# Float64 weights to fp32: exponent and mantissa by floating-point arithmetic, or a shifted upper word plus an integer addition

## The chip, the core and the metric

The kernel runs on one core of a Trainium2 chip. That core has TensorE (matrix products; PE in the profile, with PEld for its weight loads), VectorE (DVE) and ScalarE (ACT) for elementwise work, GpSimd (POOL), and SyncE (SP), which here issues DMA transfers between HBM and the on-chip memory SBUF. The metric is the device time of one execution in microseconds; lower is better.

## What is computed

An attention block without a softmax feeds a two-layer network. In short:

```python
# q, k, v: (8 batches, 8 heads, 576 rows, 64)
kv  = einsum('bhsd,bhse->bhde', k, v)
o   = einsum('bhsd,bhde->bhse', q, kv)
x   = o / sqrt(mean(o*o, -1) + 1e-6) * g_norm        # then (4608 tokens, 512)
h   = x @ w_in                                       # (4608, 2048)
g   = h * erf(softplus(h))
out = g @ w_out                                      # (4608, 512), fp32
```

`w_in` (512 x 2048) and `w_out` (2048 x 512) arrive as **float64**. [...] each weight reaches the kernel as two 32-bit words, and the kernel makes an fp32 number out of them. The change is in that step alone.

## The kernel before

The tokens are worked off in nine groups (512 rows of each of the eight batches, and a last group with the 64 rows left of each); group T=0 begins while the weights are still being fetched. The weights come in 18 pieces, in the order in which they are needed: four of `w_in` with 128x512 numbers, six of `w_in` and eight of `w_out` with 128x1024. Each piece is loaded raw (`load_w`), taken apart (`w_split`) and put together (`w_join`); the plan of the program places these three steps between the other work.

A float64 has a sign bit, 11 exponent bits and 20 mantissa bits in its upper word, and 32 mantissa bits in its lower word. The kernel before builds two factors: `e`, an fp32 power of two with the sign, and `m`, an fp32 number from 1 to 2; their product is the weight.

```python
    def w_split(which, f, k):
        hi = w_raw[which, f].rearrange("p (n two) -> p n two", two=2)[:, :, 1]
        e = early.tile([P, G * k], I32, name="w_e", tag="w_e", bufs=2)
        m = early.tile([P, G * k], I32, name="w_m", tag="w_m", bufs=2)
        nc.vector.tensor_scalar(out=e, in0=hi, scalar1=20, scalar2=0x7FF,          # L207
            op0=ALU.logical_shift_right, op1=ALU.bitwise_and)
        nc.scalar.activation(e, e, AF.Relu, scale=float(1 << 23), bias=exp_col)    # L215
        nc.vector.tensor_scalar(out=m, in0=hi, scalar1=0xFFFFF, scalar2=None,      # L216
            op0=ALU.bitwise_and)
        nc.scalar.activation(m.bitcast(FP32), m, AF.Identity, scale=2.0**-20, bias=1.0)  # L219
        w_cv[which, f] = e, m

    def w_join(which, f, k):
        # hi, lo: the upper and lower words of the raw piece, every second word
        nc.vector.scalar_tensor_tensor(out=e, in0=hi, scalar=-(1 << 31), in1=e,    # L226
            op0=ALU.bitwise_and, op1=ALU.bitwise_or)
        nc.vector.scalar_tensor_tensor(out=m, in0=lo, scalar=2.0**-52, in1=m,      # L230
            op0=ALU.mult, op1=ALU.add)
        nc.vector.tensor_tensor(out=out_, in0=e, in1=m, op=ALU.mult)               # L240
```

(Written more tightly than in the kernel; `out_` is the piece's place in `w_in_sb` or `w_out_sb`.) The plan around the first group, cut:

```python
    w_rounds = {
        1: ("split",),
        2: ("join", "load", "split"),
        3: ("join", "load"),
        5: ("split",),
        6: ("split", "join", "load", "join", "load"),
    }
    ...
    for i in range(NP + 3):                       # NP = 4 pairs of heads
        for piece, p in ((0, i), (1, i - 1), (4, i - 3), (3, i - 2)):
            if 0 <= p < NP:
                first[p][piece]()                 # 0 products, 1 apply, 3 mean, 4 norm of pair p
        if i == 1:
            for _ in range(RAW - 2):
                w_next("load")
            ...
        for what in w_rounds.get(i, ()):
            w_next(what)
```

The norm of a head pair, whose lines stand between the conversion's in the profile:

```python
            nc.scalar.activation(r, ms, AF.Ln, bias=eps_col)                       # L358
            nc.scalar.activation(r, r, AF.Exp, scale=-0.5)                         # L359
            nc.scalar.activation(u, r, AF.Square)                                  # L360
            ...
            nc.vector.scalar_tensor_tensor(out=u, in0=ms, scalar=EPS, in1=u,       # L366
                op0=ALU.add, op1=ALU.mult)
            nc.vector.scalar_tensor_tensor(out=u, in0=u, scalar=3.0, in1=r,        # L369
                op0=ALU.subtract, op1=ALU.mult)
            ...
            nc.vector.scalar_tensor_tensor(out=x, in0=st.pop("o"), scalar=gm_col,  # L378
                in1=u, op0=ALU.mult, op1=ALU.mult)
```

The hidden products that take the converted weights, block by block (blocks 0 and 1 together, then one by one):

```python
                nc.tensor.matmul(plain[i],                                         # L692
                    lhsT=w_in_sb[:, c, i % FC * P : i % FC * P + P],
                    rhs=xT[T][:, c, :], start=(c == 0), stop=(c == KC - 1))
```

Of the kernel before, what the change touches and what calls it, by code (L numbers as in the profile page):

```python
# [39 lines left out]
FP32 = mybir.dt.float32  # L40
FP32R = mybir.dt.float32r
I32 = mybir.dt.int32
U32 = mybir.dt.uint32
AF = mybir.ActivationFunctionType
ALU = mybir.AluOpType
# [15 lines left out]
def kernel(  # L61
# [10 lines left out]
    nc = tc.nc  # L72
    P = 128
# [11 lines left out]
    const = ctx.enter_context(tc.tile_pool(name="const", bufs=1))  # L85
# [67 lines left out]
    for i in range(2):  # L153
        nc.gpsimd.dma_start(
            out=g_col[i * D : i * D + D, :], in_=g_norm.rearrange("(d one) -> d one", one=1)
# [16 lines left out]
    for i in range(2):  # L172
        nc.vector.memset(mean_f[i * D : i * D + D, i * D : i * D + D], 1.0 / D)
    nc.vector.tensor_copy(out=mean_w, in_=mean_f)
    exp_col = const.tile([P, 1], FP32, name="exp_col")
    nc.vector.memset(exp_col, -896.0 * (1 << 23))
    eps_col = const.tile([P, 1], FP32, name="eps_col")
    nc.vector.memset(eps_col, EPS)
    bd_kv = const.tile([P, 2, P], FP32, name="bd_kv")
# [6 lines left out]
    w_raw, w_cv = {}, {}  # L186
    RAW = 4

    def load_w(which, f, k):
# [6 lines left out]
        else:  # L196
# [2 lines left out]
                in_=moe_w_out.rearrange("(t p) f -> p t f", p=P)[:, f : f + k, :],  # L199
            )  # L200

    def w_split(which, f, k):

        hi = w_raw[which, f].rearrange("p (n two) -> p n two", two=2)[:, :, 1]
        e = early.tile([P, G * k], I32, name="w_e", tag="w_e", bufs=2)
        m = early.tile([P, G * k], I32, name="w_m", tag="w_m", bufs=2)
        nc.vector.tensor_scalar(  # L207
            out=e,
            in0=hi,
            scalar1=20,  # L210
            scalar2=0x7FF,
            op0=ALU.logical_shift_right,
            op1=ALU.bitwise_and,
        )
        nc.scalar.activation(e, e, AF.Relu, scale=float(1 << 23), bias=exp_col)  # L215
        nc.vector.tensor_scalar(  # L216
            out=m, in0=hi, scalar1=0xFFFFF, scalar2=None, op0=ALU.bitwise_and
        )
        nc.scalar.activation(m.bitcast(FP32), m, AF.Identity, scale=2.0**-20, bias=1.0)  # L219
        w_cv[which, f] = e, m  # L220

    def w_join(which, f, k):
        raw, (e, m) = w_raw.pop((which, f)), w_cv.pop((which, f))
        hi = raw.rearrange("p (n two) -> p n two", two=2)[:, :, 1]
        lo = raw.bitcast(U32).rearrange("p (n two) -> p n two", two=2)[:, :, 0]
        nc.vector.scalar_tensor_tensor(  # L226
            out=e, in0=hi, scalar=-(1 << 31), in1=e, op0=ALU.bitwise_and, op1=ALU.bitwise_or
        )
        m = m.bitcast(FP32)
        nc.vector.scalar_tensor_tensor(  # L230
            out=m, in0=lo, scalar=2.0**-52, in1=m, op0=ALU.mult, op1=ALU.add
        )
        e = e.bitcast(FP32)
        if which == "in":
            out_ = w_in_sb[:, :, f * P : (f + k) * P]
            e, m = (t.rearrange("p (c f) -> p c f", c=KC) for t in (e, m))
        else:
            out_ = w_out_sb[:, f : f + k, :]
            e, m = (t.rearrange("p (c f) -> p c f", c=k) for t in (e, m))
        nc.vector.tensor_tensor(out=out_, in0=e, in1=m, op=ALU.mult)  # L240


    w_order = sorted(
# [6 lines left out]
    def w_next(what):  # L250
        i = w_at[what]
        if i < len(w_order):
            w_at[what] = i + 1
            {"load": load_w, "split": w_split, "join": w_join}[what](*w_order[i][1:])
# [389 lines left out]
    for n in range(FIRST * FC + 1):  # L644
        T, f = divmod(n, FC)
# [108 lines left out]
    def part(h, half):  # L754
        return h[:, :, half * 2 * P : half * 2 * P + 2 * P]
# [31 lines left out]
    for m in range(first_batch, batches + 1):  # L787
# [73 lines left out]
        for j in range(J):  # L861
# [13 lines left out]
            for half in due_halves:  # L875
                nc.vector.tensor_tensor(  # L876
                    out=part(h, half), in0=part(h, half), in1=part(s, half), op=ALU.mult
# [38 lines left out]
```

## Time and profile before

| | |
|---|---|
| time, median of 3 runs | 944.46 us (944.22 to 944.83) |
| span of the profiled execution | 942.4 us |
| conversion, first raw word read to last weight written | 14.4 to 125.0 us |
| VectorE operations of the conversion | 18 each of L207, L216, L226, L230, L240 |
| ScalarE operations of the conversion | 18 each of L215, L219 |

In the profile a line such as L207 is a line of the kernel before; `out<-in` names the tiles written and read. The chain that ended last follows, from the last instruction backwards, what released each instruction; time on it is time that sets the end. The clock that TensorE was granted was 1.00 in every stretch of the span.

### The profile page before, as it was taken

The page shows a single profiled execution, that of the slowest core. Times are in us where ns is not written, and L with a number is a line of the kernel's source. Part 1 is how long each engine was busy: PE and PEld are TensorE (multiplying, and loading weights), DVE is VectorE, ACT ScalarE, POOL GpSimd, SP SyncE. Part 2 cuts the span into 40 slices and gives each one's busy share as a digit, 9 for nine tenths or more (in the row PEclk, how much of TensorE's full clock was granted, in tenths as well). Part 3 has the DMA queues.
Part 4 walks back from the last instruction along what each step waited for, and adds up shares of the span by engine and source line. Part 5 has one row for each costly group of instructions (what it writes and reads, how often), then busy time and mean ns, then how long its engine had stood idle before and what let it go on. Part 6 is the DMA issues. An engine that isn't in the chain of part 4 may idle for free.

```text
span 942.4 us, 11743 instructions
## 1 busy us (share of the span) xinstructions
PE 924.8 (98%) x4272; PEld 683.4 (73%) x4272; DVE 742.6 (79%) x1056; ACT 615.6 (65%) x825; POOL 2.4 (0%) x10
## 2 busy tenths in 40 slices
PE   6999999999999999999999999999999999999997
PEld 4444445666688888888888888888888888888886
DVE  3999858887577787877778888878887877787667
ACT  3899776776766666666666666666666666665551
POOL 1000000000000000000000000000000000000000
PEclk9999999999999999999999999999999999999999
DMA  9766406899699998998899889998896778778871
GB/s 257 276 204 207 150 1 227 318 351 335 214 363 335 309 325 283 306 311 307 280 287 314 294 298 309 311 303 296 293 325 260 263 253 345 284 286 287 353 263 46
DMA packets 111842, 259.78 MB, mean 276 GB/s; under 512 B 43864, under 2 KB 69544, under 8 KB 111784
## 3 DMA queue, kind: packets, MB, share of 16 engines
q1 hardware_dynamic: 110152, 256.73, 78.7%
q10 hardware_dynamic: 1568, 2.29, 0.8%
q8 instruction: 34, 0.56, 0.2%
q14 instruction: 24, 0.20, 0.1%
q0 software_dynamic: 64, 0.00, 0.0%
HBM read 224.40 MB, written 34.60 MB: 275 GB/s over the span
## 4 chain that ended last, share of the span: by engine, by line
PE 92%; DVE 4%; DMA 2%; ACT 1%; issue 0%; SPq 0%; DVEq 0%
PE n_ps L462 45%; PE m_ps L462 22%; PE o_ps L520 10%; PE h_ps L692 6%; PE se_ps L325 3%; PE kv_ps L297 2%; PE qt_ps L319 2%; DMA w_raw<-in_moe_w_in_dram 1%; PE ms_ps L351 1%; DMA v_sb<-in_v_dram 1%; DVE h L876 1%; DVE e L445 1%; PE ms_ps L346 1%; PE ms_ps L347 1%; PE kv_ps L324 1%; DVE e L440 0%
## 5 line engine op out<-in xcount | busy, mean ns | idle before, releaser
L462 PE MATMUL n_ps<-x_forms,w_in_parts 128*128 128x512 f32 x896 | 232.5, 401 | 0.1
L462 PE MATMUL n_ps<-w_out_parts,g_forms 128*128 128x512 f32 x928 | 231.2, 391 | 0.0
L462 PEld LDWEIGHTS n_ps<-w_out_parts,g_forms 128*128 128x128 f32 x928 | 174.2, 188 | 38.4 <-issue 1.4
L462 PEld LDWEIGHTS n_ps<-x_forms,w_in_parts 128*128 128x128 f32 x896 | 166.8, 188 | 43.1 <-issue 9.3
L852 ACT ACTIVATE s<-h 128x512 f32<-128x512 f32 x112 | 71.0, 633 | 178.9 <-DVE h L445 178.9
L445 DVE TENSOR_TENSOR h<-m_ps,h 128x512 f32<-128x512 f32 x116 | 79.7, 687 | 59.8 <-ACT h L837 43.8
L462 PE MATMUL m_ps<-w_out_parts,g_forms 128*128 128x512 f32 x464 | 124.2, 389 | 0.0
L462 PE MATMUL m_ps<-x_forms,w_in_parts 128*128 128x512 f32 x448 | 120.0, 390 | 0.0
L520 PE MATMUL o_ps<-w_out_sb,h_sb 128*128 128x512 f32 x224 | 100.8, 593 | 0.3 <-DVE h_sb L642 0.3
L462 PEld LDWEIGHTS m_ps<-w_out_parts,g_forms 128*128 128x128 f32 x464 | 87.1, 188 | 18.0
L462 PEld LDWEIGHTS m_ps<-x_forms,w_in_parts 128*128 128x128 f32 x448 | 84.1, 188 | 17.7
L445 DVE TENSOR_TENSOR e<-m_ps,e 128x512 f32<-128x512 f32 x116 | 80.2, 692 | 18.2 <-PE m_ps L462 10.9
L440 DVE SCALAR_TENSOR_TENSOR e<-n_ps,e 128x512 f32<-128x512 f32 x88 | 60.3, 685 | 39.2 <-PE n_ps L462 39.2
L520 PEld LDWEIGHTS o_ps<-w_out_sb,h_sb 128*128 128x128 f32 x224 | 42.3, 190 | 48.9 <-issue 46.6
L411 DVE SCALAR_TENSOR_TENSOR g_forms<-g_forms 128x1024 fp32r<-128x1024 f32 x58 | 71.1, 1225 | 2.0
L408 DVE TENSOR_TENSOR g_forms<-h,g_forms 128x1024 fp32r<-128x1024 f32 x58 | 70.6, 1217 | 1.7 <-ACT g_forms L405 1.4
L876 DVE TENSOR_TENSOR h<-h,s 128x1024 f32<-128x1024 f32 x58 | 68.3, 1218 | 0.7 <-ACT s L856 0.7
L837 ACT ACTIVATE h<-n_ps 128x512 f32<-128x512 f32 x112 | 65.5, 585 | 3.4 <-PE n_ps L462 3.4
L405 ACT ACTIVATE g_forms<-h 128x1024 fp32r<-128x1024 f32 x58 | 58.9, 1059 | 12.2 <-PE m_ps L462 8.7
L692 PE MATMUL h_ps<-xT,w_in_sb 128*128 128x512 f32 x144 | 64.9, 594 | 0.7 <-DVE w_in_sb L240 0.6
L106 ACT ACT_TABLE_LOAD x44 | 56.5, 1283 | 0.8
L856 ACT ACTIVATE s<-s 128x1024 f32<-128x1024 f32 x56 | 56.2, 1052 | 0.3
(98 smaller groups left out, 1013.3 us busy)
## 6 DMA issues: line engine op xcount, KB each, us to landing
w_out_parts<-w_out SPq DMA_DIRECT2D x116, 768.0 KB
w_in_parts<-w_in SPq DMA_DIRECT2D x112, 768.0 KB
w_in<-w_new SPq DMA_DIRECT2D x16, 768.0 KB
q_sb<-in_q_dram SPq DMA_DIRECT2D x32, 256.0 KB
w_raw<-in_moe_w_out_dram SPq DMA_DIRECT2D x8, 1024.0 KB
out_dram<-e SPq DMA_DIRECT2D x32, 256.0 KB
k_sb<-in_k_dram SPq DMA_DIRECT2D x28, 287.5 KB
v_sb<-in_v_dram SPq DMA_DIRECT2D x28, 287.5 KB
```

The lines of the kernel that those rows point to most:

```text
L106: nc.scalar.preload_act_table_set("softplus")
L405: nc.scalar.activation(high, x, AF.Copy, scale=1.0 + 2.0**-13)
L408: nc.vector.tensor_tensor(out=low, in0=x, in1=high.bitcast(FP32), op=ALU.subtract)
L411: nc.vector.scalar_tensor_tensor(out=both, in0=low.bitcast(FP32), scalar=SHIFT, in1=high.bitcast(FP32), op0=ALU.mult, op1=ALU.add,)
L440: nc.vector.scalar_tensor_tensor(out=out_, in0=ps, scalar=scale, in1=out_, op0=ALU.mult, op1=ALU.add)
L445: nc.vector.tensor_tensor(out=out_, in0=ps, in1=out_, op=ALU.add)
L462: nc.tensor.matmul(ps, lhsT=weights(form, k), rhs=moving(form, k), start=(form == forms[0] and k == 0), stop=(form == forms[-1] and k == 3),)
L520: nc.tensor.matmul(o_ps[j], lhsT=g[:, j * P : j * P + P], rhs=w_out_sb[:, f, :], start=(f == 0), stop=last,)
L692: nc.tensor.matmul(plain[i], lhsT=w_in_sb[:, c, i % FC * P : i % FC * P + P], rhs=xT[T][:, c, :], start=(c == 0), stop=(c == KC - 1),)
L837: nc.scalar.activation(h[:, i], n_ps, AF.Copy, scale=SHIFT - 1.0)
L852: nc.scalar.activation(s[:, i], h[:, i], AF.Softplus)
L876: nc.vector.tensor_tensor(out=part(h, half), in0=part(h, half), in1=part(s, half), op=ALU.mult)
```

## The change

The exponent of an fp32 has 8 bits instead of 11, with another offset, and its mantissa has 23 bits. The changed kernel uses that an fp32 multiplication by a power of two moves the exponent's offset: it takes the upper word as if it were an fp32 number, multiplies by 2^-112 on ScalarE, shifts the result left by 3 bits on VectorE, and sets the sign bit from the upper word. This is the weight cut to 20 mantissa bits. The lower word is scaled by 2^-29 on ScalarE and rounded to an integer, the last three bits with their rounding; one 32-bit integer addition puts them in, and a carry from the mantissa runs on into the exponent as it should. What the change is for: fewer operations on VectorE (three for each piece instead of five), no wait of ScalarE for VectorE, and one rounding.

```diff
--- before.py
+++ after.py
@@ -172,8 +172,6 @@
     for i in range(2):
         nc.vector.memset(mean_f[i * D : i * D + D, i * D : i * D + D], 1.0 / D)
     nc.vector.tensor_copy(out=mean_w, in_=mean_f)
-    exp_col = const.tile([P, 1], FP32, name="exp_col")
-    nc.vector.memset(exp_col, -896.0 * (1 << 23))
     eps_col = const.tile([P, 1], FP32, name="eps_col")
     nc.vector.memset(eps_col, EPS)
     bd_kv = const.tile([P, 2, P], FP32, name="bd_kv")
@@ -199,45 +197,44 @@
                 in_=moe_w_out.rearrange("(t p) f -> p t f", p=P)[:, f : f + k, :],
             )
 
+    def words(which, f):
+
+        raw = w_raw[which, f]
+        hi, lo = (
+            raw.bitcast(kind).rearrange("p (n two) -> p n two", two=2)[:, :, half]
+            for kind, half in ((FP32, 1), (U32, 0))
+        )
+        return hi, lo, raw.rearrange("p (n two) -> p n two", two=2)[:, :, 1]
+
     def w_split(which, f, k):
 
-        hi = w_raw[which, f].rearrange("p (n two) -> p n two", two=2)[:, :, 1]
+
+        hi, lo, _ = words(which, f)
         e = early.tile([P, G * k], I32, name="w_e", tag="w_e", bufs=2)
         m = early.tile([P, G * k], I32, name="w_m", tag="w_m", bufs=2)
+        nc.scalar.activation(e.bitcast(FP32), hi, AF.Copy, scale=2.0**-112)
+        nc.scalar.activation(m, lo, AF.Copy, scale=2.0**-29)
+        w_cv[which, f] = e, m
+
+    def w_join(which, f, k):
+
+
+        hi = words(which, f)[2]
+        e, m = w_cv.pop((which, f))
+        w_raw.pop((which, f))
         nc.vector.tensor_scalar(
-            out=e,
-            in0=hi,
-            scalar1=20,
-            scalar2=0x7FF,
-            op0=ALU.logical_shift_right,
-            op1=ALU.bitwise_and,
-        )
-        nc.scalar.activation(e, e, AF.Relu, scale=float(1 << 23), bias=exp_col)
-        nc.vector.tensor_scalar(
-            out=m, in0=hi, scalar1=0xFFFFF, scalar2=None, op0=ALU.bitwise_and
-        )
-        nc.scalar.activation(m.bitcast(FP32), m, AF.Identity, scale=2.0**-20, bias=1.0)
-        w_cv[which, f] = e, m
-
-    def w_join(which, f, k):
-        raw, (e, m) = w_raw.pop((which, f)), w_cv.pop((which, f))
-        hi = raw.rearrange("p (n two) -> p n two", two=2)[:, :, 1]
-        lo = raw.bitcast(U32).rearrange("p (n two) -> p n two", two=2)[:, :, 0]
+            out=e, in0=e, scalar1=3, scalar2=None, op0=ALU.logical_shift_left
+        )
         nc.vector.scalar_tensor_tensor(
             out=e, in0=hi, scalar=-(1 << 31), in1=e, op0=ALU.bitwise_and, op1=ALU.bitwise_or
         )
-        m = m.bitcast(FP32)
-        nc.vector.scalar_tensor_tensor(
-            out=m, in0=lo, scalar=2.0**-52, in1=m, op0=ALU.mult, op1=ALU.add
-        )
-        e = e.bitcast(FP32)
         if which == "in":
             out_ = w_in_sb[:, :, f * P : (f + k) * P]
             e, m = (t.rearrange("p (c f) -> p c f", c=KC) for t in (e, m))
         else:
             out_ = w_out_sb[:, f : f + k, :]
             e, m = (t.rearrange("p (c f) -> p c f", c=k) for t in (e, m))
-        nc.vector.tensor_tensor(out=out_, in0=e, in1=m, op=ALU.mult)
+        nc.vector.tensor_tensor(out=out_.bitcast(I32), in0=e, in1=m, op=ALU.add)
 
 
     w_order = sorted(
```

The loads, the places of the three steps in the plan, the buffers (four raw pieces, two each of `w_e` and `w_m`) and all other work stay as they are.

More of the change, by code (lines that the diff above doesn't have):

```diff
@@ L200, in load_w @@
             )
+    def words(which, f):
[5 more added lines that the diff above has]
+        return hi, lo, raw.rearrange("p (n two) -> p n two", two=2)[:, :, 1]
     def w_split(which, f, k):
-        hi = w_raw[which, f].rearrange("p (n two) -> p n two", two=2)[:, :, 1]
+        hi, lo, _ = words(which, f)
         e = early.tile([P, G * k], I32, name="w_e", tag="w_e", bufs=2)
         m = early.tile([P, G * k], I32, name="w_m", tag="w_m", bufs=2)
-        nc.vector.tensor_scalar(
-            out=e,
-            in0=hi,
-            scalar1=20,
-            scalar2=0x7FF,
-            op0=ALU.logical_shift_right,
-            op1=ALU.bitwise_and,
-        )
-        nc.scalar.activation(e, e, AF.Relu, scale=float(1 << 23), bias=exp_col)
-        nc.vector.tensor_scalar(
-            out=m, in0=hi, scalar1=0xFFFFF, scalar2=None, op0=ALU.bitwise_and
-        )
-        nc.scalar.activation(m.bitcast(FP32), m, AF.Identity, scale=2.0**-20, bias=1.0)
+        nc.scalar.activation(e.bitcast(FP32), hi, AF.Copy, scale=2.0**-112)
+        nc.scalar.activation(m, lo, AF.Copy, scale=2.0**-29)
         w_cv[which, f] = e, m
     def w_join(which, f, k):
-        raw, (e, m) = w_raw.pop((which, f)), w_cv.pop((which, f))
-        hi = raw.rearrange("p (n two) -> p n two", two=2)[:, :, 1]
-        lo = raw.bitcast(U32).rearrange("p (n two) -> p n two", two=2)[:, :, 0]
+        hi = words(which, f)[2]
+        e, m = w_cv.pop((which, f))
+        w_raw.pop((which, f))
+        nc.vector.tensor_scalar(
+            out=e, in0=e, scalar1=3, scalar2=None, op0=ALU.logical_shift_left
+        )
         nc.vector.scalar_tensor_tensor(
```

## The prediction

> **What bounds the kernel now.** I read the page's busy table first, then stretches of the span, then the chain that ended last in the only stretch where TensorE is not full, then what each operation of the weight conversion costs there.
>
> ```profile
> PE 924.8 (98%) x4272; PEld 683.4 (73%) x4272; DVE 742.6 (79%) x1056; ACT 615.6 (65%) x825; POOL 2.4 (0%) x10
> ```
>
> TensorE is busy for 98% of the span. The conversion ends at 125 us, so the question is where before that TensorE is idle. The busy time by stretch (columns: stretch, length, then PE, PEld, DVE, ACT, POOL, granted clock, DMA share, GB/s):
>
> ```profile
> 0.00:20.00 20.00, 10.72 (x96) 7.58 (x96) 5.20 (x21) 5.67 (x9) 2.39 (x10) 1.00 0.95 250
> 20.00:36.00 16.00, 13.94 (x59) 6.32 (x59) 15.15 (x30) 14.71 (x24) 0.00 (x0) 1.00 0.71 224
> 36.00:60.00 24.00, 24.00 (x79) 11.26 (x80) 22.61 (x30) 21.32 (x29) 0.00 (x0) 1.00 0.89 298
> 90.00:125.00 35.00, 35.00 (x106) 16.05 (x105) 32.41 (x40) 24.91 (x32) 0.00 (x0) 1.00 0.43 134
> ```
>
> There are three regimes. Up to 20 us the DMA queues are at 0.95 and everything waits for q, k and v. From 20 to 36 us VectorE (15.15 of 16.00) and ScalarE (14.71) are full. From 36 us TensorE is busy for the whole of each stretch; 60 to 90 and 125 to 238 us read the same way, 30.00 of 30.00 and 113.00 of 113.00. VectorE is nearly full there too (22.61 of 24.00), but it does not hold TensorE up. So only 20 to 36 us can give anything. The chain there (start, duration, engine, tile, line):
>
> ```profile
> 30.50 0.34 DVE w_e L207
> 30.84 0.33 DVE w_m L216
> 31.17 0.61 DVE qT L366
> ...
> 32.53 0.75 DVE xT L378
> 33.29 0.33 DVE w_e L207
> 33.62 0.34 DVE w_m L216
> 33.95 0.61 DVE w_e L226
> 34.57 0.61 DVE w_m L230
> ...
> 35.20 0.70 DVE w_in_sb L240
> 35.90 0.04 issue
> 35.95 7.13 PE h_ps L692 x16
> ```
>
> The chain lies on VectorE without a break from 21.81 us: the norms of the four head pairs (L366, L369, L378) with conversion steps between them. At 35.95 us TensorE starts the matmuls of hidden block 2, released by the conversion of weight block 2. Two waits matter: TensorE's last matmuls of blocks 0 and 1 wait for the last norm, and block 2 then waits for its weight, with TensorE idle for 0.62 us:
>
> ```profile
> PE h_ps L692 <- DVE w_in_sb L240: 0.6, 1, 0.6
> ```
>
> The conversion's operations on a 128x512 block, by shape (busy, mean ns, idle before):
>
> ```profile
> L226 DVE SCALAR_TENSOR_TENSOR w_e<-w_raw,w_e 128x512 int32<-128x512 int32 x4 | 2.7, 686 | 0.0
> L230 DVE SCALAR_TENSOR_TENSOR w_m<-w_raw,w_m 128x512 f32<-128x512 uint32 x4 | 2.7, 686 | 0.0
> L240 DVE TENSOR_TENSOR w_in_sb<-w_e,w_m 128x512 f32<-128x512 f32 x4 | 2.8, 692 | 0.1
> L207 DVE TENSOR_SCALAR w_e<-w_raw 128x512 int32<-128x512 int32 x4 | 1.7, 418 | 0.0
> L215 ACT ACTIVATE w_e<-w_e,exp_col 128x512 int32<-128x512 int32 x4 | 2.9, 715 | 0.9 <-DVE w_e L207 0.9
> L219 ACT ACTIVATE w_m<-w_m 128x512 f32<-128x512 int32 x4 | 2.5, 614 | 0.0
> ```
>
> Durations overlap: successive VectorE operations start 0.34 us (L207, L216) and 0.61 us (L226, L230) apart in the chain.
>
> [...] 418 ns (L207) against 692 ns (L240) for 512 elements. [...] In the changed program's instruction list it is indeed an instruction of its own kind, whose output counts 4x256 for a block of 4x128: 16-bit halves, unit stride. [...] I estimate the old multiplication's time, 0.69 us. No trace here shows it yet.
>
> [...] L215 with its bias column takes 715 ns, the Copy of x into its upper part (L405, 128x512) 629 ns.
>
> [...] The new ScalarE steps read every second word. [...] L207 reads every second word in 418 ns, the cast at L338 contiguous ones in 420 ns. No ScalarE operation in the trace before reads with that stride.
>
> **The change part by part.** Per block the two tensor_scalars on VectorE (L207, L216) and the lower-word multiply-add (L230) go; one in-place tensor_scalar (the shift) comes, now in the joining part; the sign step stays; the multiplication becomes the integer addition. ScalarE keeps two operations, now straight from the raw words: they wait for the DMA, not for VectorE. TensorE's order and DMA sizes stay.
>
> VectorE's busy time falls by 14 x (0.69 + 1.22) + 4 x (0.42 + 0.69) = 31 us (one tensor_scalar and one multiply-add net, for 14 blocks of 128x1024 and 4 of 128x512). Nearly all of it lies after 36 us or before 20 us, beside a full TensorE or the DMA queues, and is worth nothing. What lies on the chain:
>
> 1. Join of block 1 at 24.23 to 26.15 us: 1.92 us. New, each step depending on the one before and so starting its duration plus 0.03 later: 0.42 + 0.03 + 0.69 + 0.03 + 0.61 = 1.78. Saves 0.14.
> 2. Tensor_scalars of block 2 at 30.50 us: 0.67 removed. The last norm starts 0.14 + 0.67 = 0.81 earlier, near 30.3 us. ScalarE's last Square for it ends at 29.54 + 0.63 = 30.17 us before, about 0.1 sooner after (the bias column goes). So VectorE stays last, with only 0.1 to 0.2 us to spare.
> 3. The last norm ends at 33.28 - 0.81 = 32.47 us. TensorE's remaining matmuls of blocks 0 and 1 took from there to 35.33 (35.95 less the idle 0.62); now to 34.52.
> 4. Tensor_scalars of block 3 at 33.29 us: 0.67 removed. Join of block 2: 33.95 to 35.90, 1.95; new 0.45 + 0.72 + 0.69 = 1.86, saves 0.09. The weight is ready at 35.90 - 0.81 - 0.67 - 0.09 = 34.33 us. ScalarE feeds it in time: table load 30.1 to 31.4, its two steps to 32.6; the shift comes at 32.5.
>
> So block 2 starts at the later of 34.52 and 34.38. VectorE gains 1.57 us, but TensorE becomes the limit, and 35.95 - 34.52 = 1.43 us remain. From there TensorE is full until 238 us; the stall there (238.0 to 248.3, a chain of VectorE and ScalarE steps after a matmul) has no conversion in it. The gain passes through: 944.46 - 1.43 = 943.0 us.
>
> **The rivals.** (a) The 31 us taken from VectorE shorten the conversion stage at large. For it: VectorE is at 22.61 of 24.00 there and ScalarE waits 7.9 us in all for L207. Against: TensorE is at 24.00 of 24.00. It would give 920 to 935 us; I give it almost nothing.
>
> (b) The strided reads run at half speed on ScalarE. The slope of L219 is (1042 - 614) / 512 = 0.84 ns per element (its means at 1024 and 512), so 14 x 2 x 0.86 = 24 us are added between 36 and 125 us, where ScalarE has 74.3 of 89 us busy (21.32 + 28.10 + 24.91): over the top, and it empties TensorE's PSUM. It would make 947 to 955 us. Against it: [...] VectorE's reads.
>
> (c) The addition runs at half speed. Add 0.53 us to step 4: ready at 34.86, gain 1.0, 943.4 us. Later blocks cost 1.1 us more each, 15 in all, less than the 31 saved.
>
> (d) Weights 4 and 5 come late. Their 1 MB is issued at 31.35 us and is there by 37.7 (no wait at the first read). ScalarE then needs 2.1 us and the end of the join 1.2 more: ready near 41.5. TensorE now wants them at 44.48 - 1.43 = 43.05. Later loads start sooner, since raw buffers come free sooner, and share the queue; a landing over 1.5 us later would eat the gain.
>
> (e) ScalarE takes over at step 2 and the gain stops at 1.2 or so.
>
> **Range and chances.** Three of the rivals, (c), (d) and (e), only cut the gain, to between 0.5 and 1.3 us; an earlier DMA release could add 0.3. The runs before lie within 0.6 us. So 942.1 to 944.3 us. A 2% move is 19 us: nothing in the stage can give it, and only a far worse (b) could cost it.
>
> **What would show it.** After: L207, L216 and L230 gone, a shift near 0.42/0.69 us and an addition near 0.69/1.23 us; ScalarE's two steps near 0.62/1.05 us; TensorE's first 16-matmul run of hidden block 2 starting near 34.5 us with hardly an idle gap; TensorE full from there to about 236.6 us. ScalarE steps of 1 us or more on 512 elements, or TensorE gaps between 36 and 125 us, would prove the prediction wrong.

## The result, and the profile after

The changed kernel takes 981.71 us (median; 979.38 to 982.03), the kernel before 944.42 in the same sitting: a ratio of 1.0383 with a 95% interval of 1.0368 to 1.0399. Predicted were 943.0 us (942.1 to 944.3). One execution was disturbed (2428.84 us) and is left out; the profile below is that of a second sitting of the same kernel, e1_after (980.98 us, ratio 1.0387 [1.0369, 1.0405]).

Busy times over the span, the line that answers to the first one of the prediction:

```profile
PE 940.4 (96%) x4272; PEld 686.7 (70%) x4272; DVE 716.7 (73%) x1019; ACT 618.0 (63%) x825; POOL 2.4 (0%) x10
```

VectorE fell by 742.6 - 716.7 = 25.9 us. (The prediction's 31 us add up single durations; added up in the same way the conversion's went from 126.4 to 95.2 us. The table counts overlapping time once.) TensorE has the same 4272 matmuls and is busy 15.6 us longer. The stretches of the conversion (length, PE, PEld, DVE, ACT, POOL, granted clock, DMA share, GB/s):

```profile
0.00:20.00 20.00, 9.07 (x89) 6.81 (x90) 2.07 (x12) 4.16 (x6) 2.40 (x10) 1.00 1.01 222
20.00:36.00 16.00, 10.79 (x56) 5.07 (x54) 13.41 (x27) 14.01 (x23) 0.00 (x0) 0.99 0.68 183
36.00:60.00 24.00, 16.34 (x49) 7.02 (x49) 6.40 (x9) 9.27 (x14) 0.00 (x0) 0.79 0.63 224
60.00:90.00 30.00, 25.23 (x79) 11.33 (x77) 15.56 (x23) 21.76 (x28) 0.00 (x0) 0.89 0.45 134
90.00:125.00 35.00, 30.57 (x88) 13.96 (x89) 19.98 (x25) 24.11 (x30) 0.00 (x0) 0.90 0.61 178
```

Between 36 and 125 us TensorE was full before. Now it is busy for 16.34 of 24, 25.23 of 30 and 30.57 of 35 us, at a granted clock of 0.79 to 0.90 instead of 1.00, and VectorE and ScalarE are emptier too: everybody waits. The list of TensorE's waits (total, times, longest) and its timeline (start, duration, operation, in brackets the idle time before it) say for what:

```profile
PE h_ps L689 <- DVE w_in_sb L237: 19.8, 5, 6.6
```

```profile
31.16 1.88 PE L689 MATMUL h_ps<-xT,w_in_sb 128*128 128x512 f32 x4
39.65 7.68 PE L689 MATMUL h_ps<-xT,w_in_sb 128*128 128x512 f32 x14 [6.61 <-DVE w_in_sb L237]
51.34 7.97 PE L689 MATMUL h_ps<-xT,w_in_sb 128*128 128x512 f32 x14 [4.01 <-DVE w_in_sb L237]
```

And the additions in VectorE's timeline:

```profile
22.21 0.69 DVE L237 CUSTOM_DVE_ANT_0 w_in_sb<-w_e,w_m 128x1024 uint16<-128x1024 uint16 x1
28.66 0.69 DVE L237 CUSTOM_DVE_ANT_0 w_in_sb<-w_e,w_m 128x1024 uint16<-128x1024 uint16 x1
37.01 0.69 DVE L237 CUSTOM_DVE_ANT_0 w_in_sb<-w_e,w_m 128x1024 uint16<-128x1024 uint16 x1
38.90 0.69 DVE L237 CUSTOM_DVE_ANT_0 w_in_sb<-w_e,w_m 128x1024 uint16<-128x1024 uint16 x1
50.06 1.23 DVE L237 CUSTOM_DVE_ANT_0 w_in_sb<-w_e,w_m 128x2048 uint16<-128x2048 uint16 x1 [0.17 <-ACT s_sb L717]
```

Read the two together. At 31.16 us TensorE begins blocks 0 and 1, whose weights are ready since 22.90 and 29.35. (The last chunk of x is ready at 35.82.) It does four matmuls and stops until 39.65, when the addition of block **3** is over. It goes on with blocks 0 and 1, and in block 2 it stops again until the addition of the piece with blocks **4 and 5** has ended (50.06 + 1.23 = 51.29; start at 51.34). Three more such waits follow, of 4.59, 2.46 and 2.15 us. TensorE waits for weights that it doesn't need yet.

The operations themselves took what was foreseen (mean ns on a 128x512 block; the addition counts 16-bit halves):

```profile
L228 DVE SCALAR_TENSOR_TENSOR w_e<-w_raw,w_e 128x512 int32<-128x512 int32 x4 | 2.8, 692 | 0.1
L237 DVE CUSTOM_DVE_ANT_0 w_in_sb<-w_e,w_m 128x1024 uint16<-128x1024 uint16 x4 | 2.8, 692 | 0.6
L215 ACT ACTIVATE w_e<-w_raw 128x512 f32<-128x512 f32 x4 | 2.6, 662 | 0.0
L216 ACT ACTIVATE w_m<-w_raw 128x512 int32<-128x512 uint32 x4 | 2.6, 655 | 0.0
```

### The profile page after: what moved, and what is told of

It is laid out like the page before. It is cut to its first block, busy times and chain, and to the rows that moved or that the text cites. A ratio compares the mean times of both kernels' runs of the same rounds, so it can differ in the third digit from the quotient of the medians.

```text
span 2427.0 us, 11746 instructions
## 1 busy us (share of the span) xinstructions
PE 2408.5 (99%) x4272; PEld 1292.1 (53%) x4272; DVE 727.2 (30%) x1019; ACT 634.8 (26%) x825; POOL 2.4 (0%) x10
## 4 chain that ended last, share of the span: by engine, by line
PE 99%; DVE 1%; DMA 1%; ACT 0%; issue 0%; DVEq 0%
PE n_ps L459 47%; PE m_ps L459 24%; PE o_ps L517 11%; PE h_ps L689 7%; PE se_ps L322 3%; PE kv_ps L294 2%; PE qt_ps L316 2%; PE ms_ps L348 1%; PE ms_ps L344 1%; PE ms_ps L343 1%; PE kv_ps L321 0%; DMA v_sb<-in_v_dram 0%; DMA q_sb<-in_q_dram 0%; PE kv_ps L302 0%; DVE w_e L228 0%; DVE w_in_sb L237 0%
## 5 line engine op out<-in xcount | busy, mean ns | idle before, releaser
L459 PE MATMUL n_ps<-x_forms,w_in_parts 128*128 128x512 f32 x896 | 585.2, 858 | 0.0
L459 PE MATMUL n_ps<-w_out_parts,g_forms 128*128 128x512 f32 x928 | 583.2, 829 | 0.0
L459 PEld LDWEIGHTS n_ps<-w_out_parts,g_forms 128*128 128x128 f32 x928 | 318.0, 343 | 234.9 <-issue 234.6
L459 PEld LDWEIGHTS n_ps<-x_forms,w_in_parts 128*128 128x128 f32 x896 | 319.8, 358 | 221.0 <-issue 218.0
L459 PE MATMUL m_ps<-w_out_parts,g_forms 128*128 128x512 f32 x464 | 302.8, 824 | 0.0
L459 PE MATMUL m_ps<-x_forms,w_in_parts 128*128 128x512 f32 x448 | 294.9, 833 | 0.0
L517 PE MATMUL o_ps<-w_out_sb,h_sb 128*128 128x512 f32 x224 | 273.4, 1435 | 0.0
L459 PEld LDWEIGHTS m_ps<-w_out_parts,g_forms 128*128 128x128 f32 x464 | 166.7, 359 | 109.7 <-issue 109.4
L689 PE MATMUL h_ps<-xT,w_in_sb 128*128 128x512 f32 x144 | 175.8, 1435 | 4.6 <-DVE w_in_sb L237 4.6
L322 PE MATMUL se_ps<-qT,bd_kv 128*128 128x512 f32 x64 | 84.6, 1403 | 0.0
```

What stands on the lines that cost most here:

```text
L322: nc.tensor.matmul(o_ps, lhsT=bd, rhs=qT, start=True, stop=True)
L459: nc.tensor.matmul(ps, lhsT=weights(form, k), rhs=moving(form, k), start=(form == forms[0] and k == 0), stop=(form == forms[-1] and k == 3),)
L517: nc.tensor.matmul(o_ps[j], lhsT=g[:, j * P : j * P + P], rhs=w_out_sb[:, f, :], start=(f == 0), stop=last,)
L689: nc.tensor.matmul(plain[i], lhsT=w_in_sb[:, c, i % FC * P : i % FC * P + P], rhs=xT[T][:, c, :], start=(c == 0), stop=(c == KC - 1),)
```

## The experiments

The kernel before took 944.3 to 944.6 us in each of the three sittings. Ratios are to the kernel before of the same sitting, with 95% intervals.

### First sitting: the clock, the instruction, or the reads?

**e1_after**, the changed kernel again.

> The changed kernel again, for a trace of an undisturbed execution. Three theories for the 37 us that it takes more. (C, clock) TensorE runs at a low rate for longer at the start: then the fp32 matmuls show more than 0.43 us each for the first 60 to 100 us, and from there the trace runs parallel to the one before; 979 to 982 us. (I, instruction) the integer-addition instruction itself costs or disturbs: the addition, or the operations right after it, show long durations or gaps of some 2 us at each of the 18 places. (S, strided reads) ScalarE's strided reads hold up other engines: long ScalarE durations between 20 and 125 us and TensorE gaps in the same stretch.

980.98 us. The loss is the kernel's own, and its trace, shown above, fits none of the three theories as written: the additions take 0.69 us, ScalarE's reads are not long (662 and 655 ns), and TensorE's clock is low in the stretches in which its waits end (0.79 between 36 and 60 us).

**e2_mult**, the changed kernel with a plain fp32 multiplication in place of the integer addition, at the same place and with the same output (ScalarE makes a factor near 1 of the lower word; the weights differ from the reference's in their last bits).

```diff
-        nc.scalar.activation(m, lo, AF.Copy, scale=2.0**-29)
+        nc.scalar.activation(m.bitcast(FP32), lo, AF.Identity, scale=0.7 * 2.0**-52, bias=1.0)
-        nc.vector.tensor_tensor(out=out_.bitcast(I32), in0=e, in1=m, op=ALU.add)
+        nc.vector.tensor_tensor(out=out_, in0=e.bitcast(FP32), in1=m.bitcast(FP32), op=ALU.mult)
```

> The changed kernel with the integer addition replaced by the built-in fp32 multiplication of the same size: ScalarE turns the lower word into 1 plus a small number, and the weight is multiplied by it (the last bits then come from an average slope and not exactly). Same number of operations and the same order, and the strided reads stay. Theory I: 943 us, as predicted for the change. Theories C and S: 979 to 982 us.

952.15 us, ratio 1.0082 [1.0067, 1.0098]. TensorE has no wait on a conversion left, and its clock over the span is 0.998 where e1_after has 0.986. So 28.8 us hang on the addition, although the multiplication lasts as long (692 ns against 692). The strided reads of ScalarE are in both and are not the cause. Some 8 us are left that no theory had.

**e3_tiny** and **e4_once**, the kernel before with integer additions of 128x8 words in a scratch tile of its own: one in each join (18), or a single one at the start.

```diff
+    tiny = const.tile([P, 2, 8], I32, name="tiny")
+    nc.vector.memset(tiny, 0)
+    nc.vector.tensor_tensor(out=tiny[:, 0], in0=tiny[:, 1], in1=tiny[:, 1], op=ALU.add)   # e4: here; e3: in w_join
```

> The kernel before, and after each of its 18 multiplications an exact integer addition of 128x8 zeros into a scratch tile. No conversion step is changed. Theory I: 18 such instructions slow it by tens of us, 960 to 985 us. Theories C and S: 944 to 946 us.

> The kernel before with one single exact integer addition of 128x8 zeros on VectorE near its start, before any matmul. If the mere presence of the instruction in the program slows it (theory I in its strongest form), 960 to 985 us; if each execution costs, 944 to 947 us; theories C and S: 944 to 945 us.

953.83 us (1.0097 [1.0082, 1.0112]) and 952.80 us (1.0092 [1.0075, 1.0109]). Neither gives the 37 us: it is not the presence of the instruction. But both lose 8 to 9 us, one addition as much as eighteen. That is the odd 8 us of e2_mult again, in a kernel that has no addition. What the three kernels have in common is that a small tile was added or taken away (e2_mult, like the change, has no `exp_col`), so the tiles placed after it moved: the buffers of q, k and v, of the raw weights and of the later weight pieces (`w_in_sb`, `w_out_sb`, `xT` and `h_sb`, which lie at the other end, did not).

### Second sitting: the range of the wait, and the addresses

Two theories came out of it. R: what is waited for is the whole stretch of `w_in_sb` between the first and the last word that an addition writes. One join writes four short rows, 2048 words apart, so its stretch covers a little more than three of the four row chunks, for all blocks. The list of waits in the built program fits: of the matmuls of a block, the one on chunk c=0, which lies ahead of the stretches of all later joins, waits for none of them; the one on c=1 waits for the latest join issued. A: the addresses of the tiles cost the rest.

The waits of TensorE's first `h_ps` matmuls in the two built programs (row, destination; each row is two of the profile's matmuls):

```
        before                                    changed
31      block 0, c=0                              block 0, c=0
33      block 0, c=1  [waits DVE]                 block 0, c=1  [waits DVE]
35      block 0, c=2  [waits DVE]                 block 0, c=2
37      block 0, c=3  [waits DVE]                 block 0, c=3
39      block 2, c=0  [waits DVE]                 block 2, c=0
40      block 2, c=1                              block 2, c=1  [waits DVE]
43      block 3, c=0  [waits DVE]                 block 3, c=0
```

Before, the waits of block 0 are those for x, chunk by chunk, and blocks 2 and 3 each wait at c=0 for their own join. In the changed program row 33 carries a wait so late (39.65 us in e1_after, where the last chunk of x is ready at 35.82) that all that would follow is covered by it, until c=1 of block 2 needs the next.

**e5_rows**, the changed kernel with the addition of each `w_in` piece as four instructions, one for each chunk, so that none writes with a gap.

```diff
-        nc.vector.tensor_tensor(out=out_.bitcast(I32), in0=e, in1=m, op=ALU.add)
+        for c in range(e.shape[1]) if which == "in" else ():
+            nc.vector.tensor_tensor(out=out_[:, c].bitcast(I32), in0=e[:, c], in1=m[:, c], op=ALU.add)
+        if which == "out":
+            nc.vector.tensor_tensor(out=out_.bitcast(I32), in0=e, in1=m, op=ALU.add)
```

> The changed kernel with the addition of each block of the first weight matrix as four instructions, one for each of the four row chunks, so that none writes with a gap. Theory R (the wait is given for the whole stretch of w_in_sb from the first to the last word that an addition writes, so TensorE waits for joins that it does not need): TensorE's idle time of 6.6, 4.0, 4.6, 2.5 and 2.2 us between 31 and 125 us goes, and its slow matmuls after them; the time falls to that of the version with a plain multiplication, 952 us (950 to 954). Rival I (the addition itself takes VectorE or TensorE too long): four instructions cost more start-up than one, 980 us or more.

952.07 us, ratio 1.0093 [1.0074, 1.0111]. Theory R held: with the same arithmetic on the same words the waits for the addition, 19.8 us in e1_after, are gone from TensorE's list, and the time is that of the multiplication (952.15).

**e6_cols**, the kernel before with `exp_col` and `eps_col` in one tile: the tiles placed after them lie 32 bytes lower, as in the changed kernel.

```diff
-    exp_col = const.tile([P, 1], FP32, name="exp_col")
-    eps_col = const.tile([P, 1], FP32, name="eps_col")
+    cols = const.tile([P, 2], FP32, name="cols")
+    exp_col, eps_col = cols[:, 0:1], cols[:, 1:2]
```

> The kernel before, with its two one-word columns exp_col and eps_col in one tile, so that every tile placed after them lies 32 bytes lower, as in the changed kernel; nothing else differs. Theory A (the 8 us that the versions without the waits still lose come from where the tiles lie): about 952 us (949 to 955). Rival F (they come from having the addition, or another new operation, in the program): 944.5 us.

954.70 us, ratio 1.0106 [1.0089, 1.0123], with not one operation changed. Theory A held.

**e7_once_in_place**, e4_once with the scratch words inside the 32 bytes that `exp_col` takes anyway (the edit, written more tightly).

```diff
-    exp_col = const.tile([P, 1], FP32, name="exp_col")
+    cols = const.tile([P, 8], FP32, name="cols")
+    exp_col, zero = cols[:, 0:1], cols.bitcast(I32)
+    nc.vector.memset(cols, 0.0)
+    nc.vector.tensor_tensor(out=zero[:, 1:4], in0=zero[:, 4:7], in1=zero[:, 4:7], op=ALU.add)
```

> The kernel before with one integer addition on three words at the start, as e4_once, but with the scratch words inside the 32 bytes that exp_col takes anyway, so that no other tile moves. Theory A (addresses): 944.5 us, where e4_once took 952.8. Rival F (the addition's presence): 952 to 953 us again.

945.03 us, ratio 1.0009 [1.0002, 1.0016]; e4_once had 1.0092. What is left, 0.7 us, is there by 36 us in the trace and doesn't grow after it.

**e8_both**, the changed kernel with both repairs: e5's four additions, and `exp_col` with its fill kept, unused.

> The changed kernel with the addition in four instructions as e5_rows, and with the tile exp_col and its fill kept, so that all tiles lie as in the kernel before. Theories R and A together: both losses go and what the prediction expected is left, 942 to 944.5 us. With R alone 952 us; with A alone 972 us; with neither 980 us.

943.34 us (942.94 to 944.94), ratio 0.9991 [0.9983, 1.0000]: the conversion as the change meant it, and the one version of the changed kernel that isn't slower than the kernel before. By the interval its gain lies between 0 and 1.6 us. Its stretches from 20 to 60 us, and TensorE's timeline there:

```profile
20.00:36.00 16.00, 14.46 (x61) 7.05 (x62) 14.25 (x33) 14.78 (x24) 0.00 (x0) 1.00 0.70 216
36.00:60.00 24.00, 24.00 (x81) 11.21 (x80) 15.87 (x28) 22.43 (x30) 0.00 (x0) 1.00 0.93 320
```

```profile
27.20 1.10 PE L353 MATMUL ms_ps<-qT,mean_w 128*128 128x512 f32 x2 [1.46 <-DVE qT L368]
28.13 13.90 PE L694 MATMUL h_ps<-xT,w_in_sb 128*128 128x512 f32 x32
```

TensorE is at 24.00 of 24.00 again, and its 32 matmuls of blocks 0 to 3 run without a gap. VectorE has 15.87 of 24.00 where it had 22.61 before: that relief is real, and worth nothing.

### Third sitting: where the address matters, and whether the losses add

In the kernel before, the buffers of q, k, v, the raw weights and the later weight pieces start at multiples of 256 bytes in each partition: the first q at 27904 = 109 x 256, the raw weights from 67840 = 265 x 256, the pieces from 85760 = 335 x 256. In the changed kernel and e6_cols they lie 32 bytes lower, in e3_tiny and e4_once 64 higher (four of the eight buffers of `w_out_parts` stay in all of them).

**e9_early64** and **e10_early256**, the kernel before with an unused tile of 64 or 256 bytes ahead of the buffers of the early pool (the second buffers of q, k, v, and the raw weights); the first buffers and everything after 250 us stay.

```diff
+    early.tile([P, 16], FP32, name="pad", bufs=1)     # e9; e10: [P, 64]
     for i in range(NP - 1):
         load_pair(i)
```

> The kernel before with an unused 64-byte tile ahead of the buffers of the early pool: the second buffers of q, k and v and all buffers of the raw weights lie 64 bytes higher, at addresses that are no longer multiples of 256; the first buffers of q, k and v and everything used after 250 us stay. Theory L (line: a transfer into SBUF is slower when its buffer doesn't start at a multiple of 256 bytes): the raw weights land later as in e6_cols, TensorE loses some of the 3 to 4 us that e6_cols lost by 48 us, and none after 250 us: 945.5 to 948 us. Rival P (only the position against other tiles, not the multiple, matters): no firm number, but then e10 loses about the same.

> As e9_early64, but the unused tile has 256 bytes, so the same buffers move and still start at multiples of 256. Theory L: 944 to 945 us, the time of the kernel before. Rival P: 945.5 to 948 us, as e9.

946.59 us (1.0022 [1.0014, 1.0029]) and 944.72 us (1.0002 [0.9994, 1.0011]). The same buffers moved further cost nothing that can be seen, if they keep a multiple of 256: theory L held. Only starts 64 above and, in e6_cols, 32 below such a multiple were tried; whether a multiple of 128 would do is not known.

**e11_late_back**, e6_cols with an unused 32-byte tile ahead of the pool used from 250 us on.

```diff
+            late.tile([P, 8], FP32, name="pad")
             forms = late.tile([P, 3, KC, G], FP32R, name="x_forms0")
```

> e6_cols (all tiles on the left 32 bytes lower), with an unused 32-byte tile ahead of the pool used from 250 us on, so that the weight pieces and forms of the second half lie as in the kernel before and only q, k, v and the raw weights are moved. If the loss of e6_cols is in both halves (3 to 4 us by 60 us, 5 us or more of slow drift of TensorE after 250 us), the drift goes and 947 to 950 us is left. If it is all made early, 952 to 955 us as e6_cols.

949.87 us, ratio 1.0058 [1.0046, 1.0071]. About half of the loss of e6_cols lies in each part. The delay of TensorE's matmuls against the same matmuls in the trace of the kernel before, in us (worked out from the starts of single matmuls; the trace of e6_cols is of its longest execution, 957.63 us):

```
matmul starting, before, at us    36     60    200    262    400    600    800    936
e6_cols                          1.3    3.2    3.1    4.4    7.4    9.4   12.8   13.8
e11_late_back                    2.1    4.0    4.1    4.1    4.2    4.3    4.4    4.4
e9_early64                       1.7    2.1    2.1    2.1    2.3    2.3    2.2    2.3
e10_early256                     0.5    0.6    0.6    0.6    0.7    0.7    0.7    0.7
e8_both                         -1.0   -1.2   -1.2   -1.2   -1.0   -1.0   -1.0   -0.9
```

The early part goes with slower transfers; which landing held which matmul was not followed up. The first ten microseconds, before, e6_cols, e9_early64, e10_early256 in this order, the last column the GB/s:

```profile
0.00:10.00 10.00, 2.85 (x29) 2.32 (x29) 1.37 (x9) 1.47 (x2) 2.39 (x10) 1.00 0.79 209
```
```profile
0.00:10.00 10.00, 2.85 (x29) 2.32 (x29) 1.37 (x9) 1.37 (x2) 2.38 (x10) 1.00 0.90 187
```
```profile
0.00:10.00 10.00, 2.85 (x29) 2.31 (x29) 1.33 (x9) 1.28 (x1) 2.39 (x10) 1.00 0.79 193
```
```profile
0.00:10.00 10.00, 2.85 (x29) 2.32 (x29) 1.37 (x9) 1.58 (x2) 2.39 (x10) 1.00 0.81 207
```

The packets of 1536 bytes (k and v of the first batch) take 85.8 ns on average before, 100.3 in e6_cols, 101.2 in e11, 98.3 in e9, 100.3 in e4_once, 89.7 in e10, 88.1 in e8 and 81.9 in e12. So they average 98.3 to 101.2 ns in the four kernels in which buffers start off a multiple of 256, 32 below it (e6_cols, e11) or 64 above it (e9, e4_once), and 81.9 to 89.7 in the four in which the buffers named above start at one. By what mechanism such a start makes a packet longer was not shown.

The late part is of another kind. Set against the same matmuls before, e6_cols loses 9.4 us after 262 us. Of these, 5.1 are waits: 19 matmuls, most of them on pieces of `w_in`, start 0.05 to 1.3 us late. The larger part of the rest, 3.9 us, is about 500 matmuls on the streamed weights that take 5 to 50 ns longer each. In e5_rows, which has the same addresses, the late loss is 6.2 us, 1.8 of them in 8 waits and again 3.8 in about 500 small delays. The group of the kernel before, then e6_cols, then e11_late_back:

```profile
L462 PE MATMUL n_ps<-x_forms,w_in_parts 128*128 128x512 f32 x896 | 232.5, 401 | 0.1
```
```profile
L462 PE MATMUL n_ps<-x_forms,w_in_parts 128*128 128x512 f32 x896 | 234.9, 404 | 2.7 <-DMA w_in_parts<-w_in 1.5 <-ACT h L837 1.1
```
```profile
L462 PE MATMUL n_ps<-x_forms,w_in_parts 128*128 128x512 f32 x896 | 232.6, 401 | 0.1
```

That putting back the late tiles removes it is shown; why matmuls lengthen and some pieces come late is not. The 6144-byte packets of those pieces have a median of 234 ns in all three and a mean that is not longer (270.7 ns before, then 262.6 and 265.5), so slower packets are not it. `x_forms0` and the pieces moved together and were not told apart.

**e12_col**, the changed kernel with `exp_col` and its fill kept, and nothing else.

> The changed kernel with the tile exp_col and its fill kept, unused, so that all tiles lie as in the kernel before; the addition stays one instruction. The two causes add (981 less the 8 to 9 us of the addresses): 971 to 974 us. If the addresses matter only where TensorE is full, the waits would swallow part of it: 975 to 981 us.

974.41 us, ratio 1.0318 [1.0304, 1.0333], between the two ranges. The addresses are worth 980.98 - 974.41 = 6.6 us where the false waits are in, and 952.07 - 943.34 = 8.7 where they are not. The two differ by no more than their intervals allow (each about 2 us wide to either side). In the traces the part after 200 us is alike, 6.2 and 6.5 us, and the part before it is 1.9 where the waits are in and 3.0 where they are not, as if a late landing could hide in a wait that is there anyway; with one trace of each this is a hint and not shown. Against e8_both, which differs by the four additions alone, it loses 31.1 us. Of these, 19.8 are TensorE's idle time for joins, and its busy time is 936.6 - 924.3 = 12.3 us longer; together 32.1, where the spans of the two traces differ by 972.8 - 941.5 = 31.3. Where the 12.3 come from is in its timeline. After the wait of 6.60 us the next matmuls start 1.01, 0.85, 0.85, 0.85 and 0.58 us apart before they are back at 0.43; after the next wait it is six at 0.85 to 1.02.

These matmuls go with the granted clock: 0.85 is twice 0.43, this lasts for 4.1 us after the first wait, and the clock is 0.50 from 33.51 to 40.34 us, where the wait ends at 36.46. The waits of 2.46 and 2.14 us bring 3.4 us at half clock each as well. What sets the start and the length of a slow stretch was not shown. Two such stretches, with the granted clock as third from last, and the matmuls after the wait of 2.46 us:

```profile
33.51:40.34 6.83, 3.88 (x5) 1.82 (x6) 2.59 (x5) 0.32 (x1) 0.00 (x0) 0.50 1.03 397
91.54:94.95 3.41, 3.41 (x7) 1.53 (x6) 0.00 (x0) 0.27 (x1) 0.00 (x0) 0.50 0.92 252
```

```profile
90.32 4.32 PE L691 MATMUL h_ps<-xT,w_in_sb 128*128 128x512 f32 x6 [2.46 <-DVE w_in_sb L239]
```

## Why the prediction was wrong

**The sum that was measured.** From the kernel before (944.31): the arithmetic in itself -0.97 (e8_both), the addresses +8.73 (e8 to e5), the false waits and the slow clock after them +28.91 (e5 to e1_after), which is 980.98. The terms are differences along one path, so they must add up; along the other one (e8 to e12_col to e1_after) the waits come to 31.07 and the addresses to 6.57. The four kernels have each cause in or out in every combination.

**The step that failed.** "TensorE's order and DMA sizes stay." They do, but a wait belongs to an instruction as its order does, and the waits had changed. From this came step 4's "block 2 starts at the later of 34.52 and 34.38" and "From there TensorE is full until 238 us". In the changed kernel blocks 0 and 1, which the prediction took as running through, stopped in their second chunk until the last join of the opening stage, and block 2 started at 46.31 us in e1_after instead of 34.52. With the four waits after it TensorE stood idle for 19.8 us, and its granted clock in the three stretches from 36 to 125 us, in which these waits end, was 0.79, 0.89 and 0.90 instead of 1.00. No rival named this. Its closing paragraph had the sign: "TensorE gaps between 36 and 125 us, would prove the prediction wrong". The gaps could have been foreseen, not from the profile but from the list of waits of the changed program, where row 40 waits and row 39 doesn't; the prediction takes from it the order and the form of the addition, and doesn't speak of the waits.

**The step that was missing.** The prediction noted that the bias column goes, and counted 0.1 us for it. It did not ask where the tiles behind it come to lie. That cost 6.6 to 8.7 us, several times the gain under discussion.

**What was right.** The durations: shift 0.42, sign 0.69, addition 0.692 on 128x512 and 1.226 on 128x1024 (0.69 and 1.23 were the author's estimate, the times of the multiplication), ScalarE's steps 0.66 and 0.655. The last two are not the "near 0.62/1.05" that was written (the larger ones take 1.14), but far from the half speed of rival (b), whose 24 us do not occur; (c) falls as well. (d) and (e) don't show in e8_both: TensorE begins block 4 at 43.29 us without a gap before it, and VectorE begins the last norm (30.59) as soon as the one before it is done. Rival (a), relief of VectorE at large, is refuted by e8_both, as it was argued: VectorE is 6.7 us freer in 24 and TensorE not a bit faster.

**What was off in size.** The gain is 0.97 us instead of 1.43 (block 2 starts 35.95 - 35.00 = 0.95 earlier in the trace of e8_both). Step 3 has the last norm end at 32.47; in e8_both it ends at 32.03 + 0.75 = 32.78, as step 1's join was sized too small: the addition starts 0.14 after the sign step has ended instead of 0.03, and four additions take 0.90 where one takes 0.69. The second join has the same addition, so step 4's weight is ready at 33.98 + 0.90 = 34.88 instead of 34.33. But neither sets the start. TensorE has worked without a gap since 27.20 us, when the first step of the second norm released it; it begins block 0 at 28.13, and 16 matmuls later, at 28.13 + 16 x 0.43 = 35.0, block 2 (35.00 in the trace). Step 3 timed "TensorE's remaining matmuls" from the end of the last norm; with that norm earlier, what came ahead of them set the end. The trace of the kernel before had this bound already:

```profile
27.96 7.36 PE L692 MATMUL h_ps<-xT,w_in_sb 128*128 128x512 f32 x16
```

27.96 + 16 x 0.43 = 34.84 is later than the predicted 34.52. What the prediction calls the stall from 238.0 to 248.3 us is a stretch in which the chain runs over VectorE and ScalarE; TensorE is busy for 10.00 of its 10.30 us.

## What to carry to other kernels

When an instruction is replaced, compare the waits of all who read or write its output, not only the order of the engines: here TensorE stood idle for 19.8 us, in five waits, for additions with a gapped output (e1_after), and not at all for the same additions in four gapless parts (e5_rows). Removing a tile of 4 bytes in each partition moved the buffers behind it by 32 bytes, and the same move cost 1.06% in e6_cols; keep the starts of transferred buffers where they were, by a pad if need be, before judging a change of 1%. And where TensorE is the bound, waits of 2 to 7 us cost more than their length here: in e12_col matmuls behind them started 0.85 us apart instead of 0.43, and 12.3 us of longer busy time came on top of 19.8 us of waits.

## What the runs showed that I had not expected

- A 32-bit integer addition is one VectorE instruction in the profile, of 692 ns for 128x512 words and 1226 for 128x1024, the same as an fp32 multiplication (692 and 1226 in e2_mult). A 128x128 part takes 286 ns.
- Tiles 32 bytes lower, with the same instructions, cost 1.06% [0.89, 1.23] (e6_cols); of two paddings of the early buffers, 64 bytes cost 0.22% [0.14, 0.29] and 256 bytes nothing that can be seen.
- That the waits cover a bounding stretch is inferred from which matmuls wait and from e5_rows, where the 19.8 us are gone; how a wait is set was not shown. Whether it is this kind of instruction, or its view of the output as 16-bit halves, that is treated so was not told apart; the plain multiplication writes the same words without it.
